# A statically planned attention and feed-forward kernel: one query pair moved behind an up pair, one matmul group re-priced in the planner, and the second tile's statistics held back

## The chip, the cores and the metric

The kernel runs on one core of a Trainium2 chip. The metric is the device time of one execution in microseconds (us); lower is better. Runs are compared as medians, and as the ratio that each set of rounds gives: the mean time of one kernel's runs over that of the other's runs of the same rounds, so not quite the ratio of the two medians. The kernel before was run again beside every group of experiments: its medians were 735.33, 735.43, 735.48, 735.41 and 735.31 us. The groups ran on different chips, so a comparison across groups (e8 with e4, say) is one across chips as well. Differences of 0.2 us between medians are therefore not read.

## The reference

For 2048 rows of 1024 features, a layernorm feeds two branches: linear attention with 32 heads, and a gated feed-forward block of width 3584. The attention output is scaled by a SiLU of the feed-forward output and added to the input.

```python
xn  = layernorm(x)                              # 2048 x 1024, no affine part
q, k, v = split(xn @ wqkv)                      # 32 heads of 32
phi = lambda t: where(t > 0, t + 1, exp(t)) + 1e-6
kv  = einsum("hsd,hse->hde", phi(k), v)
z   = phi(k).sum(over rows)
o   = einsum("hqd,hde->hqe", phi(q), kv) / (einsum("hqd,hd->hq", phi(q), z) + 1e-6)
s   = o @ wo
g   = silu((silu(xn @ w_gate) * (xn @ w_up)) @ w_down)
out = x + s * g
```

## The kernel before

The kernel is not written engine by engine. It declares operations with what they read, write and cost. A planner then simulates all engines with those costs and fixes **one order of instructions for each engine before anything runs**. In the traces VectorE keeps to its order: if its next instruction waits, what stands behind it waits as well (in e9 below for 1.64 us).

```python
class Plan:
    def schedule(self):
        # ... deadlines o.dl are computed backwards from TensorE's cumulated cost
                else:                                    # ACT, DVE, POOL, SP
                    rdy = [o for o in a if o.ready <= t] # ready in the SIMULATED time
                    o = min(rdy, key=lambda o: (o.dl - o.boost, o.idx)) if rdy else min(a, key=lambda o: (o.ready, o.dl))
        # ... o.done = s + o.busy + o.lat

        def mm_cost(mms):
            return sum(max(r.shape[-1] / 2400.0 + 0.0026, 0.03) for (_, _, r, _, _) in mms)
```

So an operation may be put ahead of another merely because the second one is not "ready" in the simulated time. A wrong cost costs no time by itself; it can produce a bad order.

The rows are worked in two halves (`p` is 0 or 1). In each half TensorE computes pairs of column blocks: two query pairs (`q`), seven gate pairs (`g`) and seven up pairs (`u`), each by a Strassen-like scheme of seven products. Its sums are VectorE work: sums of weight blocks (seen in the profile as `W<-W`, `X<-W`, all 16-bit), additions into PSUM that the next product of the pair needs (`ps<-ps,TM`), and after each up pair sums of hidden blocks (`H<-H`, called H sums below).

```python
        def ln_tile(i):                                  # layernorm of a tile of 128 rows
            # ...
            dve([s.r], [sA], lambda h: h.bn_stats(stats[:, j, 0, :], xa[:, 0:512]), 512)
            dve([s.r], [sB], lambda h: h.bn_stats(stats[:, j, 1, :], xa[:, 512:1024]), 512)
            dve([sA, sB], [mvr], lambda h: h.bn_aggr(mv[:, j, :], stats[:, j, :, :]), 60)
            dve([mvr], [ver], lambda h: h.tensor_scalar(veps[:, j, :], mv[:, j, 1:2], EPS_LN, None, ALU.add), 60)
            pool([ver, nh_r], [rsr], lambda h: h.tensor_tensor(rstd[:, j, :], veps[:, j, :], neg_half[:, :], ALU.pow), 0.56)
            # ... then (x - mean) * rstd, transposed on TensorE for the first tiles

        def recip(p):                                    # denominators of the attention
            for g in range(NG):
                for q in range(4):                       # 8 x 4 = 32 matmuls, each with 32 output rows
                    mms.append((ps[db][32 * q:32 * q + 32, 0:256], Zh[:, g, :], o[:, (q % 2) * 256:(q % 2) * 256 + 256], g == 0, False))
            pe_mm(rd, [bank_r[db]], mms)
            # ... four reciprocals on VectorE, result written to DRAM
        # normalise_part(p, j, half): reads the reciprocals back from DRAM spread over partitions
        # (4 transfers of 128 KB each), one ACT pass and one multiply per block, writes q to DRAM

        order = [("q", 0), ("g", 0), ("q", 1), ("u", 0)] + [(k, n) for n in range(1, NPAIR // 2) for k in "gu"]
        # ...
                if p == 0 and (k, n) in (("g", 0), ("q", 1), ("u", 0)):
                    at = {"2_0": [build_m], "6_0": [build_m], "2_1": [build_m] * 2, "6_1": [build_m] * 2}
                if (k, n) == ("g", 1):
                    at = {"2_1": [partial(recip, p)]}
                if (k, n) in (("u", 1), ("g", 2)):
                    at = {w: [partial(normalise_part, p, "ug".index(k), h)] for h, w in enumerate(("2_1", "7_1"))}
```

Of the kernel before, what the change touches and what calls it, by code (L numbers as in the profile page):

```python
# [10 lines left out]
ALU = mybir.AluOpType  # L11
# [209 lines left out]
def build_kernel(nc, A_x, A_wqkv, A_wo, B_w_gate, B_w_up, B_w_down, out, WINDOW=6, NWARM=14, NPE=4, LEAD=12.0):  # L221
    S, D, FF = 2048, 1024, 3584
    NT, KT, NG, NPAIR = 16, 8, 8, 14
    EPS_LN, EPS_PHI = 1e-5, 1e-6
# [9 lines left out]
    with ExitStack() as es:  # L234
# [17 lines left out]
        def sbt(name, shape, dt):  # L252
            return es.enter_context(nc.sbuf_tensor(name, shape, dt))

        def named(*key):
            return Region([key])
# [13 lines left out]
        stats = sbt("stats", [128, 4, 2, 6], F32)  # L270
        mv = sbt("mv", [128, 4, 2], F32)
        veps = sbt("veps", [128, 4, 1], F32)
# [49 lines left out]
        MM = 0.2137  # L322

        def mm_cost(mms):
            return sum(max(r.shape[-1] / 2400.0 + 0.0026, 0.03) for (_, _, r, _, _) in mms)

        def pe_mm(reads, writes, mms):
            return PL.op("pe", reads, writes, partial(_mm_group, mms), mm_cost(mms))
# [10 lines left out]
        def act(reads, writes, o, i, func, src="ps", **kw):  # L339
            return PL.op("act", reads, writes, lambda h: h.activation(o, i, func, **kw),  # L340
                         nel(o) / 1200.0 + (0.055 if src == "ps" else 0.095))

        def dve(reads, writes, fn, n, rate=0.96):
            return PL.op("dve", reads, writes, fn, n / (rate * 1000.0) + 0.07)
# [40 lines left out]
        def pool(reads, writes, fn, busy=0.3):  # L385
            return PL.op("pool", reads, writes, fn, busy)
# [55 lines left out]
        def combos(v):  # L442
            tt([v["R11"][1], v["R01"][1]], [v["T3"][1]], v["T3"][0], v["R11"][0], v["R01"][0], ALU.subtract, True)
            tt([v["R01"][1], v["R00"][1]], [v["T1"][1]], v["T1"][0], v["R01"][0], v["R00"][0], ALU.subtract, True)
            tt([v["R11"][1], v["T1"][1]], [v["T2"][1]], v["T2"][0], v["R11"][0], v["T1"][0], ALU.subtract, True)
            tt([v["R10"][1], v["T2"][1]], [v["T4"][1]], v["T4"][0], v["R10"][0], v["T2"][0], ALU.subtract, True)
# [184 lines left out]
            dma([], [r], ap, wqkv_v[:, 4 * k:4 * k + 4, c0:c0 + 512], dsem("wkv%d%d%d" % (w, j, k)), 512 * KB)  # L631

        xnslot = {}

        def ln_tile(i):
            j = i % 4
            s = xslot[i]
            xa = s.ap()
            sA, sB, mvr, ver, rsr, nmr = (named(n, j) for n in ("sA", "sB", "mv", "ve", "rs", "nm"))
            dve([s.r], [sA], lambda h: h.bn_stats(stats[:, j, 0, :], xa[:, 0:512]), 512)  # L640
            dve([s.r], [sB], lambda h: h.bn_stats(stats[:, j, 1, :], xa[:, 512:1024]), 512)  # L641
            dve([sA, sB], [mvr], lambda h: h.bn_aggr(mv[:, j, :], stats[:, j, :, :]), 60)
            dve([mvr], [ver], lambda h: h.tensor_scalar(veps[:, j, :], mv[:, j, 1:2], EPS_LN, None, ALU.add), 60)
            pool([ver, nh_r], [rsr], lambda h: h.tensor_tensor(rstd[:, j, :], veps[:, j, :], neg_half[:, :], ALU.pow), 0.56)  # L644
            o = xn_ring.take()
            xnslot[i] = o
            oa = o.ap(FP16)
            if i < 2:
                dve([s.r, mvr, rsr], [o.r], lambda h: h.tensor_scalar(
                    oa, xa, mv[:, j, 0:1], rstd[:, j, :], ALU.subtract, ALU.mult), 1024, 2.6)  # L650
            else:
                dve([mvr, rsr], [nmr], lambda h: h.scalar_tensor_tensor(
                    nmean[:, j, :], mv[:, j, 0:1], -1.0, rstd[:, j, :], ALU.mult, ALU.mult), 60)
                act([s.r, nmr, rsr], [o.r], oa, xa, ACT.Identity, "sb", bias=nmean[:, j, :], scale=rstd[:, j, :])
# [144 lines left out]
        for n, (fn, args) in enumerate(((x_load, (0,)), (x_load, (1,)), (wkv_load, (0, 1, 0)), (wkv_load, (0, 1, 1)),  # L799
# [3 lines left out]
            k = len(PL.ops)  # L803
            fn(*args)
            for o in PL.ops[k:]:
                o.urgent = 60.0 - 2 * n
        ln_tile(0)
        t_tile(0)
        ln_tile(1)
# [68 lines left out]
        for q, kb in enumerate(kvb):  # L878
            n = 3 if q < 2 else 2
# [4 lines left out]
        for g in range(NG):  # L884
            kvp = kv_ap(g)
            dve([bank_r[kvb[g // 3]], zi_r, mask_r], [H.reg(32 * KB + g * 256, 256)],
                lambda h, g=g, kvp=kvp: h.scalar_tensor_tensor(
                    KVZ[:, g, :], kvp[:, 0:128], zinv[:, g:g + 1], maskbd[:, :], ALU.mult, ALU.mult), 128)
# [134 lines left out]
        def q_pair(p, s, stats, at, go=True):  # L1023
            stat, jstat = stats

            def evac(w):
                def f(i, j, ap, r, bank):
                    g = 2 * (2 * s + w) + i
                    o, orr = pq_tile(g, j)
                    phi_evac(ap, r, o, orr, "ps" if bank is not None else "sb")  # L1030
                return f
            s0, s1 = (xset(stat, w, XV[p], evac(w), d_ring) for w in range(2))
            pair = Pair(s0, s1, joint_of(jstat, s0, s1) if QJ[p][s] else None, at)
            if go:
                feed(pair)
            return pair
# [70 lines left out]
        def gu_pair(p, kind, n, stats, at):  # L1107
            stat, jstat = stats

            def ev_g(w):  # L1110
                def f(i, j, ap, r, bank):
                    s = sg_ring.take()
                    sgs[w, i, j] = s
                    act([r], [s.r], s.ap(FP16), ap, ACT.Silu, "ps" if bank is not None else "sb")
                return f

            def ev_u(w):
                def f(i, j, ap, r, bank):
                    s = sgs[w, i, j]
                    o, orr = hb(2 * n + w, "R%d%d" % (i, j))  # L1120
                    act([r], [orr], o, ap, ACT.Identity)
                    tt([orr, s.r], [orr], o, o, s.ap(FP16), ALU.mult, True)
                    if w == 1 and (i, j) == (1, 0):
                        h_sums(2 * n)
                return f

            def direct(w):
                def f(i, j, b, s5):
                    s = sgs[w, i, j]
                    o, orr = hb(2 * n + w, "R%d%d" % (i, j))  # L1130
                    tt([bank_r[b], s5.r], [orr], o, ps[b][:, :], s5.ap(F32), ALU.add)
                    tt([orr, s.r], [orr], o, o, s.ap(FP16), ALU.mult, True)
                return f
            s0, s1 = (xset(stat, w, XV[p], (ev_g if kind == "g" else ev_u)(w), d_ring) for w in range(2))
            if kind == "u":
                s0.direct, s1.direct = direct(0), direct(1)
            feed(Pair(s0, s1, joint_of(jstat, s0, s1), at))
# [8 lines left out]
        def pq_load(p):  # L1146
            for j in range(2):
                for k in range(2):
                    v, vr = xblock(X, 2 * j + k)
                    dma([named("q", p, k, j)], [vr], v, q_scr[p, k, j].rearrange(  # L1150
                        "p (g t) -> p g t", t=512), dsem("pql%d%d" % (k, j)), 512 * KB)
            combos(QV)
# [158 lines left out]


        combos(XV[0])
        order = [("q", 0), ("g", 0), ("q", 1), ("u", 0)] + [(k, n) for n in range(1, NPAIR // 2) for k in "gu"]
        lq = deque([(k, p, n) for p in range(2) for k, n in order])
        got = {}
        gate = [0]
# [1 line left out]
        def pump(n):  # L1319
            while lq and len(got) < n and lq[0][1] <= gate[0]:  # L1320
                k, p, s = lq.popleft()
                got[k, p, s] = q_load(p, s) if k == "q" else gu_load(k, s)
# [24 lines left out]
        for p in range(2):  # L1347
            for k, n in order:
                st = got.pop((k, p, n))
                at = {}  # L1350
                if (p, k, n) == (0, "q", 0):
                    at = {"5_1": [kv_done], "3_0": [kvt]}
                if p == 0 and (k, n) in (("g", 0), ("q", 1), ("u", 0)):
                    at = {"2_0": [build_m], "6_0": [build_m], "2_1": [build_m] * 2, "6_1": [build_m] * 2}
                if (k, n) == ("g", 1):
                    at = {"2_1": [partial(recip, p)]}
                if (k, n) in (("u", 1), ("g", 2)):
                    at = {w: [partial(normalise_part, p, "ug".index(k), h)] for h, w in enumerate(("2_1", "7_1"))}
                if last_pair[0] is not None and (p, k, n) == (1, "q", 0):
                    pass  # L1360
                elif k == "q":
                    q_pair(p, n, st, at)
                else:
                    gu_pair(p, k, n, st, at)
                if (p, k, n) == (0, "q", 0):
                    x_inner(XV[0])
                pump(1)
            feed(None)
            pq_load(p)
            for c in range(4):  # L1370
                Sx = wd_load(c)
                ms = m_load(c)
                d_set(p, c, Sx, ms)
# [69 lines left out]
```

## Time and profile before

| what | before |
|---|---|
| time, median of 4 runs | 735.33 us (735.14 to 735.49) |
| span of the profiled run | 733.8 us |
| TensorE busy | 717.2 us, 98% |
| VectorE busy | 596.9 us, 81% |
| ScalarE busy | 397.1 us, 54% |
| first matmul on real data | 8.72 us |

The busy table on the page of the kernel before (engine, busy us, share of the span, instructions):

```profile
PE 717.2 (98%) x3894; PEld 365.8 (50%) x3894; DVE 596.9 (81%) x1395; ACT 397.1 (54%) x743; POOL 14.1 (2%) x35
```

98% looks as if nothing were left. The groups by form of the kernel before (columns: line, engine, operation, out from in, shapes, count, busy us and mean ns of one, idle before) show why that reading is worth little:

```profile
L210 PE MATMUL ps<-X,W 128*128 128x512 f16 x1168 | 287.7, 379 | 1.8 <-DVE ps L347 1.6
...
L210 PE MATMUL ps<-H,Zh 128*32 128x256 bf16 x64 | 2.1, 274 | 0.0
```

A 128x512 matmul is recorded as lasting 379 ns. But twelve in a row, in the timeline of the kernel before (start us, duration us, ...), take 2.75 us from the first start to the last end:

```profile
96.49 2.75 PE L210 MATMUL ps<-H,W 128*128 128x512 f16 x12
```

(2.75 - 0.379) / 11 is 0.2155 us from start to start. Records overlap, so TensorE is "busy" even while it starves a little. The Trainium skill warns of the same ("Perfetto Trace Analysis", section Identifying the Most-Contended Engine): matmul busy time is no measure of distance from the limit, since matmuls are pipelined. It says that pipelined instructions look smaller in the trace; here a record (379 ns) is longer than the time from start to start (216 ns).

I use another measure below and call it **loss**: in a stretch of 10 us, the matmuls of each form times their pitch (the time from start to start in this trace: 0.2158 us for 512 columns, 0.1091 for 256, 0.056 for 128; with 32 output rows a quarter of the pitch of the same width), subtracted from 10 us. In a dense stretch this gives -0.38, because matmuls that straddle an edge are counted twice. I add 0.38 so that dense means 0. The counts come from groups by form in a window. Two rows of the windows view of the kernel before (start and end, length, busy us and count of PE, PEld, DVE, ACT, POOL, then clock, DMA share, GB/s) show a stretch that loses and one that does not:

```profile
480.00:490.00 10.00, 8.14 (x58) 4.35 (x51) 9.96 (x27) 4.73 (x11) 0.00 (x0) 1.00 0.08 26
640.00:650.00 10.00, 10.00 (x48) 4.48 (x47) 8.51 (x18) 2.89 (x5) 0.00 (x0) 1.00 0.45 106
```

All 48 matmuls of 640:650 are 512 wide: 48 x 0.2158 is 10.36, loss 0. The 58 of 480:490 hold 24 of 512, 22 of 256 and 12 small ones: 7.9 us of work, loss 2.5.

Three places matter. First the head, in the timeline of the kernel before:

```profile
3.76 0.69 DVE L640 BATCH_NORM_STATS2 stats<-W 128x6 f32<-128x512 bf16 x1 [2.56 <-DMA W<-in_A_x_dram]
...
4.37 0.68 DVE L641 BATCH_NORM_STATS2 stats<-W 128x6 f32<-128x512 bf16 x1
...
4.96 0.68 DVE L640 BATCH_NORM_STATS2 stats<-W 128x6 f32<-128x512 bf16 x1
...
5.55 0.19 DVE L642 BATCH_NORM_AGGREGATE mv<-stats 128x2 f32<-128x12 f32 x1
5.66 0.64 DVE L641 BATCH_NORM_STATS2 stats<-W 128x6 f32<-128x512 bf16 x1
...
6.22 0.14 DVE L643 TENSOR_SCALAR veps<-mv 128x1 f32<-128x1 f32 x1
...
6.44 0.56 POOL L644 TENSOR_TENSOR rstd<-veps,neg_half 128x1 f32<-128x1 f32 x1 [2.48 <-DVE veps L643]
...
7.03 1.17 DVE L649 TENSOR_SCALAR W<-W,mv,rstd 128x1024 f16<-128x1024 bf16 x2 [0.30 <-POOL rstd L644]
...
8.72 1.04 PE L210 MATMUL ps<-H,X 128*128 128x512 bf16 x4 [0.47 <-ACT X L340]
```

The statistics of tile 0 (3.76, 4.37) and tile 1 (4.96, 5.66) alternate with the aggregate of tile 0 (5.55). The variance of tile 0 is out at 6.37, though its own statistics ended near 5.0.

Second, the stretch after the denominator product of the second half (`Zh`), in the timeline of the kernel before:

```profile
479.26 1.06 PE L210 MATMUL ps<-H,Zh 128*32 128x256 bf16 x32
479.39 0.67 DVE L347 TENSOR_TENSOR W<-W 128x1024 f16<-128x1024 bf16 x1
...
480.93 1.41 DVE L347 TENSOR_TENSOR H<-H,TM 128x512 f16<-128x512 f16 x4
...
482.27 1.40 DVE L347 TENSOR_TENSOR H<-H 128x1024 f16<-128x1024 f16 x2
...
483.79 0.69 DVE L347 TENSOR_TENSOR ps<-ps,TM 128x512 f32<-128x512 f32 x1
...
484.54 1.04 PE L210 MATMUL ps<-X,W 128*128 128x512 f16 x4 [1.09 <-DVE ps L347]
```

The 32 matmuls take 1.06 us. From then on VectorE does weight sums, multiplications of hidden blocks and 1.4 us of H sums. The addition into PSUM (`ps<-ps,TM`) comes at 483.79, and TensorE has by then run out of anything to do: it idles 1.09 us for that addition.

Third, one matmul of the build of the projection matrix (`ps<-H`) that waits 1.27 us for ScalarE, behind a 1.28 us activation-table load:

```profile
136.82 1.28 ACT L340 ACT_TABLE_LOAD   x1
...
137.12 0.38 PE L210 MATMUL ps<-H 128*128 128x512 bf16 x1
...
138.77 0.88 PE L210 MATMUL ps<-H 128*128 128x512 bf16 x3 [1.27 <-ACT TM L340]
```

### The profile page before, as it was taken

How to read it: one execution, taken by the hardware profiler on the slowest of the kernel's cores; microseconds unless marked ns; L12 is line 12 of the kernel's file. 1: busy time of each engine (PE TensorE's matmuls, PEld its weight loads, DVE VectorE, ACT ScalarE, POOL GpSimd, SP SyncE). 2: the span in 40 equal slices, each digit the busy share in tenths (PEclk: the TensorE clock that was granted, in tenths of full speed). 3: DMA queues.
4: the chain of work that ended last, by engine and by line, in shares of the span. 5: the costliest groups of instructions: out<-in, count | busy, mean ns of one | idle time of the engine just before them, and what ended most of it. 6: DMA issues, size and time to landing. Idle time of an engine off the chain costs nothing.

```text
span 733.8 us, 10527 instructions
## 1 busy us (share of the span) xinstructions
PE 717.2 (98%) x3894; PEld 365.8 (50%) x3894; DVE 596.9 (81%) x1395; ACT 397.1 (54%) x743; POOL 14.1 (2%) x35
## 2 busy tenths in 40 slices
PE   8999999999999999999999999989999999999996
PEld 3444445455555555544444455545455554444442
DVE  6999868979899988787457889999998988757353
ACT  3776654786688565623232377666965654223231
POOL 2111000000000000000000000000000000000000
PEclk9999999999999999999999999999999999999999
DMA  8453235134276232471846535134735245264822
GB/s 292 108 104 86 44 111 175 59 116 162 73 222 203 93 103 71 128 216 33 211 116 156 167 86 151 59 103 124 238 116 172 72 137 166 78 166 115 179 65 50
DMA packets 135219, 94.00 MB, mean 128 GB/s; under 512 B 32512, under 2 KB 131072, under 8 KB 135168
## 3 DMA queue, kind: packets, MB, share of 16 engines
q1 hardware_dynamic: 135168, 93.34, 44.5%
q8 instruction: 30, 0.49, 0.3%
q14 instruction: 21, 0.17, 0.1%
HBM read 75.50 MB, written 10.62 MB: 117 GB/s over the span
## 4 chain that ended last, share of the span: by engine, by line
PE 80%; DVE 11%; ACT 7%; issue 1%; DMA 0%; POOL 0%; ACTq 0%; DVEq 0%
PE ps L210 79%; DVE W L347 3%; ACT TM L340 3%; ACT H L340 2%; DVE ps L347 2%; DVE H L347 2%; DVE TM L347 1%; DVE H L710 1%; ACT L340 1%; ACT ps L340 1%; DVE stats L640 1%; DVE TM L709 1%; DVE stats L641 0%; DMA W<-in_A_x_dram 0%; POOL rstd L644 0%
## 5 line engine op out<-in xcount | busy, mean ns | idle before, releaser
L210 PE MATMUL ps<-X,W 128*128 128x512 f16 (+1 forms) x1408 | 312.1, 361 | 2.5 <-DVE ps L347 1.6
L340 ACT ACTIVATE TM<-ps 128x512 f16<-128x512 f32 (+2 forms) x337 | 181.8, 556 | 161.1 <-PE ps L210 154.2
L210 PE MATMUL ps<-H,W 128*128 128x512 f16 (+1 forms) x896 | 206.8, 379 | 0.3 <-DVE ps L347 0.3
L210 PEld LDWEIGHTS ps<-X,W 128*128 128x128 f16 (+1 forms) x1408 | 136.4, 98 | 123.7 <-DVE ps L347 3.7
L347 DVE TENSOR_TENSOR W<-W 128x256 f16<-128x256 f16 (+6 forms) x424 | 170.4, 441 | 8.0 <-DMA W<-in_B_w_down_dram 6.0
L347 DVE TENSOR_TENSOR ps<-ps,TM 128x256 f32<-128x256 f32 (+1 forms) x218 | 117.6, 541 | 32.7 <-PE ps L210 31.6
L210 PEld LDWEIGHTS ps<-H,W 128*128 128x128 f16 (+1 forms) x896 | 87.2, 98 | 103.4 <-DVE ps L347 0.7
L340 ACT ACTIVATE ps<-ps 128x512 f32<-128x512 f32 (+1 forms) x156 | 78.9, 506 | 55.1 <-PE ps L210 50.6
L340 ACT ACTIVATE H<-ps 128x512 f16<-128x512 f32 (+1 forms) x126 | 75.2, 603 | 57.1 <-PE ps L210 56.8
L210 PE MATMUL ps<-P,W 128*128 128x256 f16 (+1 forms) x440 | 89.5, 323 | 0.6 <-ACT ps L340 0.5
L210 PE MATMUL ps<-W 128*128 128x256 f16 (+1 forms) x328 | 70.0, 299 | 1.6 <-DVE ps L347 1.1
L347 DVE TENSOR_TENSOR TM<-ps,TM 128x512 f32<-128x512 f32 (+1 forms) x60 | 40.9, 682 | 31.1 <-PE ps L210 31.0
L340 ACT ACTIVATE TM<-TM 128x512 f16<-128x512 f32 (+1 forms) x61 | 37.8, 620 | 42.7 <-DVE TM L347 41.7
L210 PEld LDWEIGHTS ps<-P,W 128*128 128x128 f16 (+1 forms) x440 | 42.9, 98 | 32.1 <-ACT ps L340 1.6
L347 DVE TENSOR_TENSOR H<-H,TM 128x512 f16<-128x512 f16 x112 | 45.6, 418 | 11.8 <-ACT H L340 11.5
L347 DVE TENSOR_TENSOR H<-H 128x1024 f16<-128x1024 f16 (+2 forms) x82 | 50.8, 631 | 1.5 <-ACT H L340 0.8
L210 PEld LDWEIGHTS ps<-W 128*128 128x128 f16 (+1 forms) x328 | 30.8, 98 | 28.9 <-DVE ps L347 2.9
L347 DVE TENSOR_TENSOR TM<-TM 128x512 f16<-128x512 f16 (+1 forms) x59 | 24.3, 420 | 18.4 <-DMA TM<-TM 10.8
L210 PE MATMUL ps<-H,X 128*128 128x512 bf16 (+1 forms) x136 | 32.2, 379 | 1.2 <-ACT X L340 0.8
L210 PE MATMUL ps<-TM,W 128*128 128x256 f16 (+1 forms) x144 | 30.9, 296 | 0.3 <-DVE ps L347 0.3
L709 DVE TENSOR_SCALAR TM<-TM 128x512 f16<-128x512 f16 x64 | 17.7, 286 | 14.3 <-ACT TM L340 14.1
L347 DVE TENSOR_TENSOR W<-H 128x1024 f16<-128x1024 f16 x40 | 26.9, 686 | 3.0 <-PE ps L210 2.7
(81 smaller groups left out, 412.9 us busy)
## 6 DMA issues: line engine op xcount, KB each, us to landing
W<-in_B_w_gate_dram SPq DMA_DIRECT2D x14, 1024.0 KB, 5.3
W<-in_B_w_up_dram SPq DMA_DIRECT2D x14, 1024.0 KB, 5.3
W<-in_B_w_down_dram SPq DMA_DIRECT2D x16, 896.0 KB, 6.3
W<-in_A_x_dram SPq DMA_DIRECT2D x16, 256.0 KB, 3.1
H<-in_A_wqkv_dram SPq DMA_DIRECT2D x8, 512.0 KB, 8.1
W<-in_A_wqkv_dram SPq DMA_DIRECT2D x4, 1024.0 KB, 5.4
H<-r_scratch SPq DMA_DIRECT2D x32, 128.0 KB, 3.7
q_scratch<-H SPq DMA_DIRECT2D x8, 512.0 KB, 3.7
```

Of the source, the lines that this page charges most:

```text
L210: last = h.matmul(o, l, r, start=st, stop=sp, skip_group_check=True)
L340: return PL.op("act", reads, writes, lambda h: h.activation(o, i, func, **kw), nel(o) / 1200.0 + (0.055 if src == "ps" else 0.095))
L347: return dve(reads, writes, lambda h: h.tensor_tensor(o, a, b, op), nel(o), 1.92 if fast else 0.96)
L640: dve([s.r], [sA], lambda h: h.bn_stats(stats[:, j, 0, :], xa[:, 0:512]), 512)
L709: dve([e.r], [b.r], lambda h: h.tensor_scalar(ba, ea, 1.0, EPS_PHI, ALU.min, ALU.add), 512, 2.6)
L710: dve([src_r, b.r], [out_r], lambda h: h.scalar_tensor_tensor(out_ap, src, 0.0, ba, ALU.max, ALU.add), 512)
```

## The change

Its stated intent: the second query pair follows the first up pair; the statistics of the second x tile wait until those of the first are complete. The diff also re-prices matmuls in the planner. In the trace the denominator product alone has fewer than 128 output rows, and none has fewer than 128 input rows, so the new factor is 1 for every other matmul. No device work is added or removed.

```diff
         def mm_cost(mms):
-            return sum(max(r.shape[-1] / 2400.0 + 0.0026, 0.03) for (_, _, r, _, _) in mms)
+            return sum(max(r.shape[-1] / 2400.0 + 0.0026, 0.03) * (o.shape[0] * r.shape[0] / 16384.0)
+                       for (o, _, r, _, _) in mms)
...
-            dve([s.r], [sA], lambda h: h.bn_stats(stats[:, j, 0, :], xa[:, 0:512]), 512)
+            o0 = dve([s.r], [sA], lambda h: h.bn_stats(stats[:, j, 0, :], xa[:, 0:512]), 512)
+            if i == 1:
+                o0.preds.add(first_var[0])
+                first_var[0].succs.append(o0)
             dve([s.r], [sB], lambda h: h.bn_stats(stats[:, j, 1, :], xa[:, 512:1024]), 512)
             dve([sA, sB], [mvr], lambda h: h.bn_aggr(mv[:, j, :], stats[:, j, :, :]), 60)
-            dve([mvr], [ver], ...)
+            o0 = dve([mvr], [ver], ...)
+            if i == 0:
+                first_var.append(o0)
...
-        order = [("q", 0), ("g", 0), ("q", 1), ("u", 0)] + ...
+        order = [("q", 0), ("g", 0), ("u", 0), ("q", 1)] + ...
...
-                if (k, n) == ("g", 1):
+                if (k, n) == ("u", 1):
                     at = {"2_1": [partial(recip, p)]}
-                if (k, n) in (("u", 1), ("g", 2)):
-                    at = {w: [partial(normalise_part, p, "ug".index(k), h)] ...}
+                if n == 2:
+                    at = {w: [partial(normalise_part, p, "gu".index(k), h)] ...}
```

So there are three separable parts: **head** (statistics), **price** (planner cost), and **reordering** (the order of the pairs, with the product and the normalising one pair later).

More of the change, by code (lines that the diff above doesn't have):

```diff
@@ L633, in build_kernel @@
         xnslot = {}
+        first_var = []
         def ln_tile(i):
@@ L639, in ln_tile @@
             sA, sB, mvr, ver, rsr, nmr = (named(n, j) for n in ("sA", "sB", "mv", "ve", "rs", "nm"))
-            dve([s.r], [sA], lambda h: h.bn_stats(stats[:, j, 0, :], xa[:, 0:512]), 512)
+            o0 = dve([s.r], [sA], lambda h: h.bn_stats(stats[:, j, 0, :], xa[:, 0:512]), 512)
+            if i == 1:
+                o0.preds.add(first_var[0])
+                first_var[0].succs.append(o0)
             dve([s.r], [sB], lambda h: h.bn_stats(stats[:, j, 1, :], xa[:, 512:1024]), 512)
             dve([sA, sB], [mvr], lambda h: h.bn_aggr(mv[:, j, :], stats[:, j, :, :]), 60)
-            dve([mvr], [ver], lambda h: h.tensor_scalar(veps[:, j, :], mv[:, j, 1:2], EPS_LN, None, ALU.add), 60)
+            o0 = dve([mvr], [ver], lambda h: h.tensor_scalar(veps[:, j, :], mv[:, j, 1:2], EPS_LN, None, ALU.add), 60)
+            if i == 0:
+                first_var.append(o0)
             pool([ver, nh_r], [rsr], lambda h: h.tensor_tensor(rstd[:, j, :], veps[:, j, :], neg_half[:, :], ALU.pow), 0.56)
@@ L1313, in build_kernel @@
         combos(XV[0])
-        order = [("q", 0), ("g", 0), ("q", 1), ("u", 0)] + [(k, n) for n in range(1, NPAIR // 2) for k in "gu"]
+        order = [("q", 0), ("g", 0), ("u", 0), ("q", 1)] + [(k, n) for n in range(1, NPAIR // 2) for k in "gu"]
         lq = deque([(k, p, n) for p in range(2) for k, n in order])
@@ L1352, in build_kernel @@
                     at = {"5_1": [kv_done], "3_0": [kvt]}
-                if p == 0 and (k, n) in (("g", 0), ("q", 1), ("u", 0)):
+                if p == 0 and (k, n) in (("g", 0), ("u", 0), ("q", 1)):
                     at = {"2_0": [build_m], "6_0": [build_m], "2_1": [build_m] * 2, "6_1": [build_m] * 2}
-                if (k, n) == ("g", 1):
+                if (k, n) == ("u", 1):
                     at = {"2_1": [partial(recip, p)]}
-                if (k, n) in (("u", 1), ("g", 2)):
-                    at = {w: [partial(normalise_part, p, "ug".index(k), h)] for h, w in enumerate(("2_1", "7_1"))}
+                if n == 2:
+                    at = {w: [partial(normalise_part, p, "gu".index(k), h)] for h, w in enumerate(("2_1", "7_1"))}
                 if last_pair[0] is not None and (p, k, n) == (1, "q", 0):
```

## The prediction

> **What bounds the kernel.** TensorE. The page's busy table gives PE 98% (717.2 us), DVE 81%, ACT 54%, but the Trainium skill ("Perfetto Trace Analysis", Identifying the Most-Contended Engine) warns that matmul busy time says little because matmuls are pipelined. The trace agrees: a 128x512 matmul lasts 379 ns in the groups by form, yet twelve of them take 2.75 us in the timeline, one per 0.216 us. I therefore counted matmuls per 10 us stretch, priced them at that pitch (256 wide: 0.109 us) and compared with a dense stretch. Losses are small and local: about 8.7 us before the first real matmul (started 8.72), 2.5 us in 10:40, 2.5 us in 130:140, 1.1 us in 180:190, 3 us in 420:470, 2.5 us in 480:490, 1.1 us in 520:530, and the tail. About 6 us of this is within the change's reach.
>
> **The change** adds and removes no device work; it changes static orders.
>
> 1. Head. Now VectorE mixes the statistics of two x tiles: variance of tile 0 ends 6.37 though its own statistics ended 4.96. Two half-statistics of tile 1 (0.59 + 0.56 us in the chain of waits) come first. After: variance about 5.2, GpSimd rstd (0.57 us) about 5.8. VectorE is then still in tile 1's second half until about 6.4, so normalise starts at 6.4 instead of 7.03: first transposes 7.0, first matmul 8.1. Weight transfers seem early enough (VectorE's first wait for them ends 8.69), and VectorE is busy about 98% from 15 to 80, so most survives: about -0.5 us.
>
> 2. The planner's price of the denominator product. It priced 32 matmuls of 32 output rows at full size, 0.109 x 32 = 3.5 us; the timeline shows 1.06 us for them (178.18 and 479.26). The Trainium skill ("TensorE: Matmul & The Clock Gate", Part 3) says such column tiles run together; 1.06 us agrees. The planner thought TensorE was 2.5 us later than it is, and put weight combinations ahead of the PSUM additions that TensorE needs: after 479 VectorE works through 1.4 us of H sums and several W sums while TensorE idles 1.09 and 0.77 us for "DVE ps". The price becomes 0.87 us. Expect the 480s loss to shrink from 2.5 to about 1 and the 180s loss from 1.1 to about 0.5: about -1.8 us.
>
> 3. Order q0 g0 u0 q1. The exponential evacuations of the two query pairs (0.28 + 0.68 us of VectorE each) are further apart, giving the 420:470 stretch some air: -0.7 us. Denominators and normalising move one pair later (four reciprocals of 0.516 us, 16 multiplies of 0.42 us and 16 ACT passes of 0.74 us each half), beside up pairs whose VectorE load is already about 91%: +0.5 us. The loss at 130:140 (projection build behind an activation-table load of 1.28 us) stays.
>
> **Sum:** -0.5 - 1.8 - 0.2 = -2.5 us: 732.9 us, range 730.0 to 735.3. All of it lies in TensorE's gaps. Chances: faster by over 2% 0.01, within 2% 0.98, slower 0.01.
>
> **Right or wrong by:** first real matmul near 8.1; TensorE idle after the Zh product under 0.5 us per wait; Zh products about one pair (12 us) later; same instruction counts; table loads 10 give or take 2; loss at 130:140 unchanged, at 420:470 down.
>
> **What would make it wrong:** the whole static order is re-simulated, so small moves elsewhere may open gaps of 1 to 2 us; reciprocals beside an up pair could stall TensorE more; the head could be held by weight transfers.

## More of the kernel before

The loss of one stretch is good to some 0.3 us, since records can be missing: the profiles of e1 to e4 and of e9 to e12 hold 3880 matmuls in place of 3894. The 14 missing ones are spread over the first 165 us, three of them between 10 and 40 us, where they add 0.65 us to the loss.

## The result, and the profile after

| | before | after |
|---|---|---|
| median of 4 runs | 735.33 us | 732.00 us (731.84 to 733.25) |
| ratio | | 0.9959, interval 0.9941 to 0.9976 |
| span of the profiled run | 733.8 us | 731.5 us |
| loss in 180:190 and in 480:490 | 1.1 and 2.5 us | 0.2 and 0.1 us |
| loss in 190:200 and in 490:500 | 0.0 and 0.2 us | 0.1 and 0.3 us |
| loss in 130:140 | 2.5 us | 2.6 us |
| loss in 420:470 | 3.0 us | 2.8 us |
| loss in 510:540 | 1.0 us | 2.5 us (1.5 in a usual run) |

The change is 3.3 us (0.45%) faster, inside the class "same within 2%". The page of the changed kernel shows that TensorE's busy time did not move at all; only the span did:

```profile
PE 717.3 (98%) x3894; PEld 365.9 (50%) x3894; DVE 596.5 (82%) x1395; ACT 397.7 (54%) x743; POOL 14.1 (2%) x35
```

The head in the timeline of the changed kernel:

```profile
3.69 0.69 DVE L642 BATCH_NORM_STATS2 stats<-W 128x6 f32<-128x512 bf16 x1 [2.49 <-DMA W<-in_A_x_dram]
...
4.30 1.27 DVE L646 BATCH_NORM_STATS2 stats<-W 128x6 f32<-128x512 bf16 x2
...
5.48 0.19 DVE L647 BATCH_NORM_AGGREGATE mv<-stats 128x2 f32<-128x12 f32 x1
...
5.71 0.15 DVE L648 TENSOR_SCALAR veps<-mv 128x1 f32<-128x1 f32 x1
5.90 0.69 DVE L642 BATCH_NORM_STATS2 stats<-W 128x6 f32<-128x512 bf16 x1
5.95 0.56 POOL L651 TENSOR_TENSOR rstd<-veps,neg_half 128x1 f32<-128x1 f32 x1 [1.99 <-DVE veps L648]
...
6.75 0.49 DVE L656 TENSOR_SCALAR W<-W,mv,rstd 128x1024 f16<-128x1024 bf16 x1
...
8.39 1.04 PE L210 MATMUL ps<-H,X 128*128 128x512 bf16 x4 [0.47 <-ACT X L341]
```

The first real matmul starts at 8.39, 0.33 us earlier. But one line answers the prediction badly: the group at 4.30 now holds **two** statistics instructions. The added dependency binds only the first half of tile 1; the planner pulled the second half of tile 1 in front of the aggregate of tile 0. Only one of the two half-statistics left the path.

The stretch after the denominator product in the second half, now at 489.70:

```profile
489.70 1.06 PE L210 MATMUL ps<-H,Zh 128*32 128x256 bf16 x32
...
491.32 0.55 DVE L1063 RECIPROCAL TM<-TM 128x64 f32<-128x64 f32 x1
491.79 0.68 DVE L348 TENSOR_TENSOR ps<-ps,TM 128x512 f32<-128x512 f32 x1
...
493.73 1.03 PE L210 MATMUL ps<-X,W 128*128 128x512 f16 x4
```

The addition into PSUM comes at 491.79, 2.1 us after the product began (before: 4.5 us), with one weight sum, two multiplications and a reciprocal ahead of it, but no H sums. TensorE's next 128x512 group at 493.73 carries no idle mark.

There is a new wait. In the timeline of the changed kernel around 520, VectorE and then TensorE wait for an up-weight block:

```profile
521.67 0.29 DVE L348 TENSOR_TENSOR W<-W 128x256 f16<-128x256 bf16 x1 [1.82 <-DMA W<-in_B_w_up_dram]
...
522.97 0.39 PE L210 MATMUL ps<-W 128*128 128x256 f16 x2 [1.33 <-DVE ps L348]
```

and the chain of waits of the same run (start us, us, what) holds that transfer, issued at 511.74, for 9.91 us, its landing (the time from issue to arrival):

```profile
511.74 9.91 DMA W<-in_B_w_up_dram
```

The median landing of the up weights is 5.5 us. In the same timeline four reads of the reciprocals were issued just before that load and eight just after it; the second profile of this kernel (e4) has the same issues, and there the load landed in 6.2 us, so the neighbours alone do not explain it. The profiled run took 733.25 us, the three others at most 732.05.

### The profile page after: what moved, and what is told of

Read it like the earlier page. It is cut to its first block, busy times and chain, and to the rows that moved or that the text cites. A ratio compares the mean times of both kernels' runs of the same rounds, so it can differ in the third digit from the quotient of the medians.

```text
span 731.5 us, 10526 instructions
## 1 busy us (share of the span) xinstructions
PE 717.3 (98%) x3894; PEld 365.9 (50%) x3894; DVE 596.5 (82%) x1395; ACT 397.7 (54%) x743; POOL 14.1 (2%) x35
## 4 chain that ended last, share of the span: by engine, by line
PE 86%; DVE 6%; ACT 4%; DMA 2%; issue 1%; POOL 0%; SPq 0%; ACTq 0%; DVEq 0%
PE ps L210 86%; ACT TM L341 2%; ACT H L341 2%; DMA W<-in_B_w_up_dram 1%; DVE H L717 1%; DVE W L348 1%; DVE ps L348 1%; DVE stats L642 1%; DVE TM L348 1%; DVE H L348 1%; ACT L341 1%; DVE TM L716 0%; DVE stats L646 0%; DMA W<-in_A_x_dram 0%; ACT ps L341 0%
```

## The experiments

Twelve kernels were run, all with a correct result and five rounds (of e3 six runs were kept, of e5 four). "Before + x" means the kernel before with only part x. How far a part reaches shows in the order of VectorE's instructions in the traces: the head changes it at 6 us alone (and nothing on TensorE), the price from 170 to 191 and from 480 to 505, the reordering from 152 to 263 and from 455 to 562. So the head can be told apart from the rest, but price and reordering work at the same places.

My theory (A): the gain is the price. A product charged 3.5 us that takes 1.06 us makes the planner believe TensorE to be 2.5 us late, so that it places ready VectorE work ahead of the additions. The rival (B): the gain comes from moving the product away from its bad neighbours, and the price is cosmetic.

| run | what | median us | range us | ratio, interval | loss 180:190 | loss 480:490 | loss 510:540 |
|---|---|---|---|---|---|---|---|
| e1 | before + head | 735.01 | 734.98 to 735.22 | 0.9994, 0.9982 to 1.0007 | 0.8 | 2.4 | 1.4 |
| e2 | before + price | 732.38 | 732.30 to 732.91 | 0.9960, 0.9948 to 0.9972 | 0.0 | 0.2 | 1.2 |
| e3 | before + reordering | 733.37 | 732.05 to 736.96 | 0.9976, 0.9959 to 0.9992 | 0.1 | 0.1 | 1.2 |
| e4 | the change again | 732.15 | 731.77 to 733.43 | 0.9958, 0.9946 to 0.9970 | 0.2 | 0.2 | 1.5 |
| e5 | before, wrong price doubled | 741.60 | 740.83 to 742.06 | 1.0082, 1.0068 to 1.0096 | 4.3 | 3.5 | 1.2 |
| e6 | before + order of pairs only | 736.89 | 736.14 to 738.11 | 1.0021, 1.0009 to 1.0034 | 2.4 | 2.4 | 1.0 |
| e7 | before + product later only | 733.64 | 732.96 to 734.55 | 0.9977, 0.9963 to 0.9990 | 0.0 | 0.0 | 1.6 |
| e8 | before + price + head | 732.13 | 731.87 to 732.54 | 0.9955, 0.9943 to 0.9968 | 0.0 | 0.0 | 1.2 |
| e9 | price + both halves wait | 734.49 | 733.28 to 734.83 | 0.9985, 0.9973 to 0.9998 | 0.2 | 0.2 | 1.1 |
| e10 | e8 + builds later | 731.54 | 730.97 to 731.80 | 0.9947, 0.9934 to 0.9961 | 0.0 | 0.1 | 1.4 |
| e11 | e9 + builds later | 732.59 | 732.36 to 732.80 | 0.9961, 0.9948 to 0.9973 | 0.0 | 0.0 | 1.3 |
| e12 | the change + builds later | 733.95 | 732.65 to 734.11 | 0.9973, 0.9959 to 0.9986 | 0.1 | 0.2 | 2.8 |

Losses are of the profiled run. In the kernels whose product comes a pair later (the change, e3, e4, e7, e12) it starts at 189.6 to 190.3 and at 489.7 to 490.5, so that the ten microseconds after it are not those of the table but 190:200 and 490:500: there they lose 0.1 to 0.2 and 0.1 to 0.4 us (the kernel before 0.0 and 0.2). Runs e1 to e4 shared the runs of the kernel before, so did e5 to e8, and e9 to e11; e12 had its own.

### e1: the head alone

```diff
+ only the lines of ln_tile and first_var of the change
```

> Only the added dependency in the statistics of the second x tile. Only eight lines of VectorE's order and four of GpSimd's differ from before; every other engine's order is the same. If the head's gain survives to the end: the first real matmul at 8.39 instead of 8.72, and the whole run shorter by the same 0.33 us (735.0). Rival: weight transfers or VectorE's later queue take it back, and the run is within 0.1 us of before although the first matmul starts earlier.

Measured 735.01 against 735.43. The first real matmul starts at 8.41, as in the changed kernel to 0.02 us. (One profile measures this start roughly: it lies at 8.5 to 8.7 in the six with the old head and at 8.2 to 8.4 in the six with the head of the change.) The median moved by 0.42 us, about what the head moved (0.31 us); the interval (0.9982 to 1.0007) includes no change, so the gain is likely but not settled by this run alone. The rival (taken back later) is not supported.

### e2: the price alone

```diff
-  sum(max(N / 2400.0 + 0.0026, 0.03) for ...)
+  sum(max(N / 2400.0 + 0.0026, 0.03) * (rows_out * rows_in / 16384.0) for ...)
```

> Only the planner's price of the 32-row product; order of the pairs and place of the product as before. Theory A (the price made the planner put VectorE work in a bad order): loss in the ten microseconds after the Zh product in the second half (480:490) falls from 2.5 us to under 0.7, in the first half (180:190) from 1.1 to under 0.5; run 2.0 to 3.0 us shorter, near 732.9. Theory B (the gain came from moving the product one pair later): the losses stay, run within 0.5 us of before.

Measured 732.38: 3.05 us faster, just above what theory A expected, and both losses are gone. The timeline of this kernel after the product of the second half, to be read against the same stretch of the kernel before:

```profile
478.82 1.06 PE L210 MATMUL ps<-H,Zh 128*32 128x256 bf16 x32
...
480.15 1.09 DVE L348 TENSOR_TENSOR H<-H,TM 128x512 f16<-128x512 f16 x3
481.16 0.69 DVE L348 TENSOR_TENSOR ps<-ps,TM 128x512 f32<-128x512 f32 x1
...
482.85 1.03 PE L210 MATMUL ps<-X,W 128*128 128x512 f16 x4
483.03 0.68 DVE L348 TENSOR_TENSOR H<-H 128x1024 f16<-128x1024 f16 x1
```

The product is at the same place (478.82, before 479.26). The addition into PSUM (481.16) now follows it by 2.3 us instead of 4.5, the H sums come after it (483.03), and the next TensorE group shows no idle mark. Same instructions, same neighbours, another order: theory B, that the price is cosmetic, is refuted.

### e3: the reordering alone

```diff
+ only the lines of `order`, `recip` and `normalise_part` of the change
```

> Order q0 g0 u0 q1 and the product and normalising one pair later, with the old price and the old head. Theory A: the wrong price still spoils the ten microseconds after the Zh product at its new place (about 190 and 491), so the run gains under 1 us. Theory B: the losses after the product are gone, the run gains 2.5 us or more (732.8 or less).

Measured 733.37: 2.06 us faster, with the losses after the product gone too (0.1 and 0.1 in the table; 0.2 and 0.3 in 190:200 and 490:500, where the product now stands). The 2.5 us that theory B expected were not reached either. So theory A, that a wrong price spoils the stretch wherever the product stands, is wrong in that form. Either part alone removes the loss; together they cannot remove it twice. The sum of e1, e2 and e3 (0.42 + 3.05 + 2.06 = 5.5 us) is far above the 3.3 us of the whole. The runs of e3 scatter more than those of any other kernel here (732.05 to 736.96); why was not found.

### e4: the changed kernel again

> The changed kernel once more, for a profile of one of its usual executions. Its profiled run took 733.25 us and the other three 731.84 to 732.05. If the 1.3 us is the late landing of one up-weight load (9.9 us, landed 521.65), this profile has TensorE's loss in 520:530 at 0.5 us or less instead of 1.7, that load landing in under 8 us, and a span near 730.2. Rival: the loss at 520:530 is in every execution, and the 1.3 us lie elsewhere.

Measured 732.15, profiled run 731.77, span 730.1. The loss in 520:530 was 0.3 us (1.7 in the first profile) and the slowest landing of the up weights 6.6 us instead of 9.9. So the late landing accounts for the difference between the two profiles of the same kernel. How often it comes is open: three of the nine runs of this kernel took over 732.5 us, and only one of them was profiled. What stays is 1.5 us in 510:540, most of it in 530:540, where the kernel before had 1.0 us, in 520:530.

### e5: the same mistake, doubled

```diff
-  sum(max(N / 2400.0 + 0.0026, 0.03) for ...)
+  sum(max(N / 2400.0 + 0.0026, 0.03) * (2.0 if rows_out < 128 else 1.0) for ...)
```

> The kernel before with the planner's price of the 32-row product doubled (7 us for a product that takes 1.06): the same mistake, twice as large. Same device work, same order of pairs, same head. If the wrong price is what makes VectorE's order bad, the loss right after the product (2.5 us in 480:490, 1.1 us in 180:190) grows: together by 1 to 4 us, run 736.5 to 739. If the price only shuffled things by luck, the run is within 0.5 us of before or even faster.

Measured 741.60: 6.1 us slower, more than expected (736.5 to 739, with 1 to 4 us of new loss), and with no device work added. The losses after the two products grew from 3.6 us together to 7.8 (and in 490:500 from 0.2 to 1.1). In the timeline of this kernel:

```profile
482.72 1.06 PE L210 MATMUL ps<-H,Zh 128*32 128x256 bf16 x32
...
489.06 0.69 DVE L348 TENSOR_TENSOR ps<-ps,TM 128x512 f32<-128x512 f32 x1
...
489.81 1.04 PE L210 MATMUL ps<-X,W 128*128 128x512 f16 x4 [2.90 <-DVE ps L348]
```

The addition comes 6.3 us after the product (4.5 with the old price, 2.3 with the new one), and TensorE idles 2.90 us for it. In the first half the delays are 6.2, 3.4 and 2.2 us. Three prices, three delays, in order: this is a cause with its dose, at this place. Not tested is by which way the price acts, by the simulated ready times or by the deadlines, for it enters both.

The delays are the dose; the 6.1 us are not all waiting. In the first half TensorE idled 2.79 us up to 185.02, and from 184.68 to 188.09 its granted clock was 0.50. A row of the windows view of this kernel (columns as above):

```profile
186.00:187.00 1.00, 1.00 (x5) 0.38 (x3) 1.00 (x3) 1.00 (x4) 0.00 (x0) 0.50 0.00 0
```

The matmuls there start 0.43 us apart in place of 0.216, so about 1.5 us of the 4.3 in 180:190 are slow clock. No other profile here has such a stretch between its first microseconds and its end, and after the idle time of 2.90 us in the second half of the same run there is none. The three runs that were not profiled have a lower mean clock (0.995, the profiled one 0.997) and are slower (741.29 to 742.06, the profiled one 740.83), which would fit more such stretches.

### e6: the order of the pairs alone

```diff
-  [("q", 0), ("g", 0), ("q", 1), ("u", 0)] + ...
+  [("q", 0), ("g", 0), ("u", 0), ("q", 1)] + ...
```

> Only the order q0 g0 u0 q1; product in the first gate pair after it as before, old price, old head. The product then follows a query pair, not an up pair, so no H sums of an up pair wait beside it. If those H sums were what VectorE did in place of the PSUM additions, the 480s loss shrinks from 2.5 to about 1 and the run is 1 to 2 us shorter; if the wrong price hurts beside any neighbour, the loss and the time stay within 0.5 us of before.

Measured 736.89: 1.4 us **slower**. (The three runs at a mean clock of 0.998 took 736.14 to 736.89, the two at 0.996 took 737.70 and 738.11.) The product now follows a query pair, and of the H sums of the up pair only one is left in front (0.69 us instead of 1.40), yet the loss in 480:490 is the same (2.4) and in 180:190 it grew from 1.1 to 2.4. My theory that the H sums are the harm fell. In the timeline of this kernel:

```profile
481.65 1.06 PE L210 MATMUL ps<-H,Zh 128*32 128x256 bf16 x32
...
482.70 2.29 DVE L347 TENSOR_TENSOR W<-W 128x256 f16<-128x256 bf16 x7
...
488.85 0.42 DVE L347 TENSOR_TENSOR ps<-ps,TM 128x256 f32<-128x256 f32 x1
...
489.33 0.39 PE L210 MATMUL ps<-W 128*128 128x256 f16 x2 [1.75 <-DVE ps L347]
```

2.29 us of weight sums stand there; the addition that TensorE needs (488.85) comes so late that it idles 1.75 us. My reading is that with the wrong price the planner fills the imagined gap with whatever is ready. No run has this order with the new price and the product at its old place, so what the order costs under a right price is not known.

### e7: the product later, alone

```diff
-  recip in ("g", 1), normalise_part in ("u", 1) and ("g", 2)
+  recip in ("u", 1), normalise_part in ("g", 2) and ("u", 2)
```

> Only the product and the normalising one pair later (product in the first up pair, which follows a gate pair), old order, old price, old head. A gate pair leaves no H sums: if they were the harm, the loss after the product (now near 491) is under 0.5 us, and the run 1.5 to 2.5 us shorter, less up to 1 us of new loss at 520:540, where the normalising now meets an up pair's weights. If the reordering of the pairs was needed, the time stays within 0.5 us of before.

Measured 733.64: 1.8 us faster, and little loss after the product (0.2 and 0.4 us in 190:200 and 490:500). With e6 this splits the reordering: the named part of the change, the order of the pairs, is a cost of 1.4 us by itself under the old price, and the gain of the reordering is the later place of the product. The timeline of this kernel shows that it is not the absence of H sums either:

```profile
490.47 1.41 DVE L347 TENSOR_TENSOR H<-H 128x1024 f16<-128x1024 f16 x2
...
492.59 0.68 DVE L347 TENSOR_TENSOR ps<-ps,TM 128x512 f32<-128x512 f32 x1
...
493.63 0.29 DVE L347 TENSOR_TENSOR W<-W 128x256 f16<-128x256 bf16 x1 [0.37 <-DMA W<-in_B_w_up_dram]
...
494.50 1.03 PE L210 MATMUL ps<-X,W 128*128 128x512 f16 x4
```

1.41 us of H sums stand right beside the product, but the addition (492.59) is still placed early, 1.9 us before the group at 494.50. VectorE then even waits 0.37 us for the up weights. What I think: at this place the weight block of the next pair had not arrived, also in the planner's simulation, so there was nothing else ready to put ahead. That is argued from these lines; no run here separates it.

### e8: price and head, without the reordering

> The changed kernel without its reordering: price and head only. The price alone gave 732.38, the head alone took 0.4 us off: if they add, 732.0, equal to the whole change (732.15) and with less scatter, because the late landing of the up weights at 520:530 belongs to the reordering. If the reordering still contributes, this is 0.5 us or more slower than the whole change.

The edit is that of e1 and e2 together. Measured 732.13, the whole change 732.15 (ratios 0.9955 and 0.9958). Once the price is right and the head is in, the reordering is worth nothing that these runs can see. Its runs scatter over 0.7 us, those of the whole change over 1.7 us. The slow landings do not belong to the reordering alone, as I had supposed: the slowest up-weight landing is 8.0 us here and 8.3 us in e2. But it was only with the reordering that landings of 9.9 and 10.5 us (the change, e12) were seen, with losses of 1.7 and 2.2 us in 520:530.

### e9: both halves of the statistics wait

```diff
             o0 = dve(... stats[:, j, 0, :] ...)
-            if i == 1:
-                o0.preds.add(first_var[0])
+            o1 = dve(... stats[:, j, 1, :] ...)
+            if i == 1:
+                for o in (o0, o1): o.preds.add(first_var[0])   # and succs
```

> Price fixed, and both half-statistics of the second x tile wait for the first tile's variance, not only the first half as in the change. Base of comparison: price and head as in the change, 732.13. The variance of tile 0 should end near 5.2 instead of 5.78, the first real matmul start near 7.9 instead of 8.39. If all of it survives: 731.6. Rival: the second weight block (VectorE's wait for it ended 8.69 to 8.85) or a worse order of the planner in 10:40 takes it back, and the run is at 732.0 or above.

Measured 734.49, which is 2.4 us slower than e8, its base, and 2.1 us slower than the price alone. The rival won. The variance of tile 0 did come earlier (5.39), but the first real matmul hardly (8.31), since VectorE was still in tile 1's statistics when rstd was ready. Then tile 1 itself came late. The timeline of this kernel:

```profile
9.10 1.22 DVE L348 TENSOR_TENSOR H<-H 128x2048 f16<-128x2048 bf16 x1 [1.64 <-DMA H<-in_A_wqkv_dram]
...
10.25 0.54 DVE L657 TENSOR_SCALAR W<-W,mv,rstd 128x1024 f16<-128x1024 bf16 x1
```

VectorE was ordered to do a sum of weight blocks first, and stood 1.64 us waiting for their transfer; the normalising of tile 1 stood behind it and started at 10.25 (7.98 in the changed kernel). The loss in 0:40 is 11.0 us against 8.1 in e8, 0.65 us of it missing records. Tile 1 explains part of the rest: TensorE idles 0.60 us for it at 10.84, but also 1.25 us at 27.06 for a normalising on ScalarE, where e8 idles 0.45 us (25.28). The 1.5 us in 140:150, where e8 has 0.2, are no further loss: it is the wait of the projection build for ScalarE (1.27 us in both), which ends at 140.81 instead of 138.42. TensorE is 2.4 us late by then, as much as the whole run. So the half-bound dependency of the change, which looks like an oversight, is better than the complete one, at least with this planner.

### e10, e11, e12: the builds of the projection matrix later

In every run so far 130:140 lost about 2.5 us (in e9 in part beyond the edge at 140), untouched by the change. These three hang the builds on later pairs.

```diff
-  if p == 0 and (k, n) in (("g", 0), ("q", 1), ("u", 0)):
+  if p == 0 and (k, n) in (("q", 1), ("u", 0), ("g", 1)):     # e10, e11; e12: u0, q1, g1
...
-  at = {"2_1": [partial(recip, p)]}
+  at = dict(at, **{"2_1": at.get("2_1", []) + [partial(recip, p)]})   # e10, e11
```

> Price and head as in the change, old order of pairs, and the sixteen builds of the projection matrix hung on the second query pair, the first up pair and the second gate pair, instead of starting in the first gate pair. The loss at 130:140 (2.5 us in every run so far, a build's matmul waiting for a bank that ScalarE frees after a 1.28 us table load) should fall under 1.2 us; run 730.5 to 731.3. Rival: the builds cost the same wherever they stand, the loss moves to 150:190 and the run stays at 732.0 or above.

> Both half-statistics waiting, and the builds later, on top of the price. If the two are independent, the run is at the price-and-head version (732.13) less the two gains of the two runs before; somewhere in 730.0 to 731.0.

> The whole change (price, head, reordering) with the builds hung on the first up pair, the second query pair and the second gate pair. Without the reordering the later builds took 0.6 us off (732.13 to 731.54). If the reordering is worth nothing once the price is right, this is within 0.4 us of 731.5; if the reordering helps when the builds are out of the first gate pair, it is at 731.0 or below; if the reordering brings its late weights at 520:530 with it, it is at 732 or above with more scatter.

e10 measured 731.54, the fastest median: 0.6 us below e8 and below both given kernels, though its interval (0.9934 to 0.9961) overlaps that of the change (0.9946 to 0.9970), so its lead over the change is likely, not settled. The wait for ScalarE is gone, but the loss in 130:140 fell only to 1.6, not under 1.2, because another wait stands there. In the timeline of e10:

```profile
134.95 0.39 PE L210 MATMUL ps<-TM,W 128*128 128x256 f16 x2 [1.11 <-DVE ps L348]
```

e11 measured 732.59, worse than e10: the harm of both halves stays when the builds move, and the expected 730.0 to 731.0 was missed. e12 measured 733.95, 1.8 us worse than the change itself: the third of its stated outcomes. Its profile has the late up weights again (slowest landing 10.5 us, TensorE idle 1.86 us) and a new loss of 1.7 us in 170:180: there a matmul of the build idles 1.36 us for ScalarE (176.37), behind a table load at 174.43. So with this order the later builds moved that wait and did not remove it.

## Why the prediction was right or wrong

The time (732.0 for 732.9 predicted, range 730.0 to 735.3) and the class were right. The steps were not all right.

- **What bounds the kernel.** Right: TensorE busy 717.2 and 717.3 us, and only gaps closed.
- **Step 1, head, -0.5 us.** Direction right, the path wrong. I predicted variance of tile 0 at 5.2 and the first matmul at 8.1; they came at 5.86 (end) and 8.39. The step that failed is "Two half-statistics of tile 1 (0.59 + 0.56 us in the chain of waits) come first. After: variance about 5.2". It assumed that both would leave. Only one did, because the dependency was added to one of two operations. Measured alone (e1): 0.31 us at the first matmul, 0.42 us in the median.
- **Step 2, price, -1.8 us.** The mechanism was right, and e2 and e5 show it. The size was the mis-sized term: alone it gave 3.05 us. I had left 1 us of loss in the 480s and 0.5 in the 180s; the runs show 0.2 and 0.0 (e2).
- **Step 3, reordering, -0.2 us net.** Near the truth by luck. In presence of the price and the head it is worth 0 (e8 against e4). By itself it is worth 2.06 us, because it removes the same loss as the price by another way; the prediction did not see that overlap. The "air" for 420:470 is there, at about half of the expected 0.7 us: the five profiles with the new order lose 2.2 to 2.8 us in that stretch (mean 2.5), the nine with the old one 2.6 to 3.0 (mean 2.9). That the order alone made the kernel 1.4 us slower lies elsewhere, in 180:190 (e6). The cost of the later normalising showed as 0.5 us (second profile) to 1.5 us (first profile) of extra loss in 510:540, for 0.5 expected; in the first profile it came through late weights, which I had not named.
- **Checks that held.** Product 10 to 11 us later (189.6 for 178.2 in the first half, 489.7 for 479.3 in the second); instruction counts equal (3894 matmuls, 1395, 743); 10 table loads in both; loss in 130:140 unchanged; TensorE's waits after the product under 0.5 us.

The sum missed by 0.8 us (-2.5 for -3.3), and nearly all of that is the price term (1.8 for 3.05 measured alone). The head, 0.1 us too large, and the reordering, 0.2 us for nothing that can be seen, took a little of the miss back.

## What to carry to other kernels

Where a planner fixes the order of instructions from costs, a wrong cost is a latent stall: it costs microseconds at one place (2.5 us of loss in 480:490) and next to nothing at another (e7), probably because no other work is ready there. So compare each price with the duration in a trace (here 3.5 us against 1.06) before moving work about. When two edits each remove the same wait, their separate gains do not add; test each with the other in place (e8) before crediting both. And when a dependency is added to hold work back, look in the trace which instruction took its place.

## What the Trainium skill lacked or had wrong

- "TensorE: Matmul & The Clock Gate", section Back-to-back issue gap: this section gives about 131 ns per matmul for a sustained stream of weight loads and 512-column matmuls, and about 216 ns for the isolated gap. Here the sustained stream with a weight load per matmul ran at 215.5 ns each (twelve in 2.75 us).
- The same page, Part 3 (packing): it measures three column tiles (2.38 times) and up to sixteen row-and-column tiles, but not four column tiles at full depth. Here 32 matmuls of 32 output rows and 256 columns took 0.99 us from first start to the start of the next group (479.26 to 480.25), 31 ns each against 109 ns for a full one, 3.5 times.
- "ScalarE: Activation LUTs", section What ACT_TABLE_LOAD costs: 1283 ns agrees to the digit (mean 1283 ns over 10). It adds about 1380 ns of drain for each switch; here the load began 0.01 us after the activation before it had ended (136.81), and the next activation started 0.02 us after the load ended (load 136.82 for 1.28, next at 138.12), so no drain shows.
- No page says that an engine's fixed order can lose time through a price: e5 lost 6.1 us with not one instruction added (about 1.5 us of it, in the profiled run, at half clock after a wait).
